# Reordered first loads, a longer last projection chunk and a shorter store wait in a one-core attention kernel

## Chip, cores, metric

One core of a Trainium2 chip. The metric is the device time of one launch in microseconds (us); several runs are timed, and the median is quoted unless something else is said. Each run has a state; every run told here was "fast", and no slow run enters a comparison. A run lists the span of its core and the mean clock granted to TensorE (PE). The time is the span plus 1.8 us. PE is TensorE, ACT ScalarE, DVE VectorE, POOL GpSimd, SP SyncE. K0, V0, K1 and so on are the K and V loads of head 0, 1 and so on; a slice is the part of Wq for one head; to evacuate is to copy a finished matmul result out of PE's accumulation banks (psA, psF, psO).

## The reference

```python
xn = layernorm(A_x)                                   # [2048, 512]
q  = xn @ wq                                          # 32 heads of 128
p  = softmax(q @ k_cache^T * 128**-0.5)               # per head, 2048 keys
s  = (p @ v_cache).concat_heads() @ wo
h  = relu(xn @ w1 + b1)**2 ;  g = silu(h @ w2 + b2)   # 1792 hidden
out = A_x + s * g
```

## The kernel before

Four query blocks of 512 rows; in each, 32 heads; in each head, 8 pairs of key tiles, 1024 pairs in all. One pair is two score matmuls (512 columns), one exponential on ACT (1.02 us) and, two pairs later, eight PV matmuls (probabilities times V, 129 columns). Between them PE gets "fillers": projections of q, the MLP and the output projection, dealt out by a credit that spreads them evenly. Loads are issued in program order by the engine that is named; SP has one queue for nearly all of them. Parts that matter (cuts marked):

```python
CH.append([(0, HC), (HC, 2 * HC), (2 * HC, 2 * HC + 4), (2 * HC + 4, H)])  # head chunks of the last block
...
ln_load(0, 0); ln_load(0, 1, AC); ln_load(0, 2); ln_load(0, 3, AC)  # x tiles, SP and ACT
fill_v(0)                       # SP
fill_wq(0, AC)
fill_k(0)                       # SP, DMA transpose
... fill_wq(1, AC); fill_wq(2, AC)
... # layernorm of 4 tiles, transposes, q of head 0
fill_k(1); fill_v(1)            # SP
for i, (c0, c1) in enumerate([(0, 4), (4, 8), (8, 11), (11, 14)]):
    ... # four pieces of W1, SP
tok_b1 = S.emit_dma(GP, ...)    # biases, issued on POOL
tok_b2 = S.emit_dma(GP, ...)
t_b1 = E(DV, partial(_copy, out=b1f[:], in_=b1b[:]), deps=[tok_b1])   # DVE waits here for b1
...
for pi in range(NPAIR):
    g, k = divmod(pi, NPR)
    gen_scores(pi)
    most = 4 if pi < 2 else 3 if k == 2 else 2      # fillers at most
    ... # fillers
    if pi >= LAG: gen_pv(pi - LAG)
    if k == 0:
        fill_wq(g + 3); fill_k(g + 2)               # at pair 0: the slice of head 3, on SP
    ...
S.emit_wait(GP, fin)            # POOL and SP both wait for the stores
S.emit_wait(SP, fin)
```

The softmax here doesn't subtract the row's maximum and nothing guards it: scores larger than these inputs give would overflow.

## Time and profile before

| | before |
|---|---|
| median (first three runs) | 1256.98 us, 1256.71 to 1257.76 |
| the profiled run | 1259.58 us, span 1257.8, granted clock 0.995 |
| PE busy | 99% of the span |

In the timeline of the kernel before (start, length of the issue, queue, line, operation, count), SP's queue holds behind K0 and K1 (the two transposes) four W1 pieces, and behind these a slice of Wq:

```profile
2.12 9.67 SPq L220 DMA_TRANSPOSE kT<-in_A_k_cache_dram  x2
...
12.46 4.76 SPq L216 DMA_DIRECT2D w_sb<-in_B_w_dram  x4
...
17.26 0.91 SPq L216 DMA_DIRECT2D wq_sb<-in_A_wq_dram  x1
```

The last line is the fourth slice, for head 3. Nobody waited for it, because PE was held up earlier by W1.

### The profile page before, as it was taken

What the parts mean: (1) busy time and instruction counts of PE and PEld (TensorE: products, weight loads), DVE (VectorE), ACT (ScalarE), POOL (GpSimd) and SP (SyncE); (2) the same over time, 40 slices, a digit from 0 to 9 for tenths busy, and PEclk for the clock granted to TensorE, in tenths of its full rate; (3) what the DMA queues carried; (4) which work ended last, traced back from release to release, by engine and by line L of the source; (5) the groups of instructions that cost most, each with busy time, mean ns of one, the idle gap of its engine ahead of it and who ended that gap; (6) DMA issues with size and microseconds to landing.
All of it is one profiled execution on the core that took longest, in us unless ns stands there. A gap on an engine that the chain in (4) does not pass through costs nothing.

```text
span 1257.8 us, 26666 instructions
## 1 busy us (share of the span) xinstructions
PE 1240.5 (99%) x11772; PEld 812.8 (65%) x11755; DVE 471.9 (38%) x946; ACT 1056.8 (84%) x1047; POOL 33.7 (3%) x78
## 2 busy tenths in 40 slices
PE   7999999999999999999999999999999999999996
PEld 3666666666666666666666666666666666666664
DVE  2543332344434333334443433233354333233342
ACT  4888888888888888888888888888888888888893
POOL 2001000000001000000000100000000000000000
PEclk8999999999999999999999999999999999999998
DMA  9999977787788887877878798787777797777760
GB/s 206 207 221 199 175 144 133 131 148 141 128 159 155 156 146 142 144 131 136 141 144 147 158 171 139 133 151 136 134 148 139 144 171 140 129 146 142 133 120 26
DMA packets 686835, 185.39 MB, mean 147 GB/s; under 512 B 675168, under 2 KB 685792, under 8 KB 686720
## 3 DMA queue, kind: packets, MB, share of 16 engines
q1 hardware_dynamic: 683408, 179.23, 78.3%
q0 software_dynamic: 1440, 3.81, 1.2%
q8 instruction: 93, 1.52, 0.5%
q10 hardware_dynamic: 1872, 0.66, 0.2%
q14 instruction: 22, 0.18, 0.1%
HBM read 96.08 MB, written 2.10 MB: 78 GB/s over the span
## 4 chain that ended last, share of the span: by engine, by line
PE 97%; DMA 1%; SPq 1%; DVE 0%; issue 0%
PE psO L157 37%; PE psA L152 35%; PE psF L152 25%; SPq L220 1%; DMA w_sb<-in_B_w_dram 1%; DMA oT<-o_bf 0%; SPq L216 0%; DVE o_un L179 0%; DVE o_bf L165 0%; DVE tmp_t L175 0%; DVE out_t L165 0%; DVE rden L191 0%
## 5 line engine op out<-in xcount | busy, mean ns | idle before, releaser
L161 ACT ACTIVATE pT<-psA 128x1024 bf16<-128x1024 f32 x1024 | 1045.4, 1024 | 177.6 <-PE psA L152 131.4
L157 PEld LDWEIGHTS psO<-v_sb,pT 128*128 128x128 bf16 x8192 | 549.3, 98 | 245.7 <-issue 17.1
L157 PE MATMUL psO<-v_sb,pT 128*128 128x129 bf16 x8192 | 635.5, 220 | 0.0
L152 PE MATMUL psA<-qt_sb,kT 128*128 128x512 bf16 x2048 | 610.0, 379 | 1.0 <-DMA kT<-in_A_k_cache_dram 1.0
L179 DVE COPY o_un<-psO 128x258 f32<-128x258 f32 x256 | 97.2, 421 | 404.9 <-PE psO L157 404.7
L152 PE MATMUL psF<-wo_all,oT 128*128 128x512 bf16 x488 | 167.9, 381 | 4.3 <-DMA oT<-o_bf 4.3
L152 PE MATMUL psF<-xnT,wq_sb 128*128 128x512 bf16 (+1 forms) x524 | 168.6, 374 | 0.2 <-ACT xnT L161 0.2
L152 PEld LDWEIGHTS psA<-qt_sb,kT 128*128 128x128 bf16 x2048 | 158.5, 98 | 1.7 <-DMA kT<-in_A_k_cache_dram 1.2
L179 DVE CAST qt_sb<-psF 128x512 bf16<-128x512 f32 (+1 forms) x129 | 88.2, 684 | 111.4 <-PE psF L152 111.4
L165 DVE TENSOR_TENSOR o_bf<-o_un,rden 128x512 bf16<-128x512 f32 x128 | 88.5, 691 | 4.9 <-DVE rden L191 0.6
L152 PEld LDWEIGHTS psF<-xnT,wq_sb 128*128 128x128 bf16 x524 | 50.7, 98 | 60.7 <-ACT xnT L161 0.3
L152 PEld LDWEIGHTS psF<-wo_all,oT 128*128 128x128 bf16 x488 | 47.7, 98 | 62.4 <-DMA oT<-o_bf 5.3
L171 DVE TENSOR_SCALAR r_t<-psF,b1f 128x512 bf16<-128x512 f32 x56 | 41.9, 748 | 109.3 <-PE psF L152 109.3
L152 PE MATMUL psF<-xnT,w_sb 128*128 128x512 bf16 x224 | 78.5, 385 | 4.4 <-DMA w_sb<-in_B_w_dram 4.4
L152 PE MATMUL psF<-w_sb,h2T 128*128 128x512 bf16 x224 | 74.3, 379 | 0.0
L152 PEld LDWEIGHTS psF<-xnT,w_sb 128*128 128x128 bf16 x224 | 22.0, 99 | 31.6 <-DMA w_sb<-in_B_w_dram 4.9
L152 PEld LDWEIGHTS psF<-w_sb,h2T 128*128 128x128 bf16 x224 | 21.9, 98 | 26.4
L165 DVE TENSOR_TENSOR acc<-psF,acc 128x512 f32<-128x512 f32 x32 | 22.0, 688 | 37.8 <-PE psF L152 37.8
L165 DVE TENSOR_TENSOR z_t<-psF,b2bc 128x512 f32<-128x512 f32 x16 | 11.1, 692 | 60.9 <-PE psF L152 60.9
L216 POOL DMA_DIRECT2D out_dram<-out_t x12 | 6.8, 565 | 889.2 <-DVE out_t L165 889.2
L165 DVE TENSOR_TENSOR h2T<-r_t 128x512 bf16<-128x512 bf16 x56 | 23.8, 425 | 1.9
L191 DVE RECIPROCAL rden<-o_un 128x4 f32<-128x4 f32 x128 | 22.8, 178 | 4.4
(41 smaller groups left out, 147.4 us busy)
## 6 DMA issues: line engine op xcount, KB each, us to landing
v_sb<-in_A_v_cache_dram SPq DMA_DIRECT2D x128, 512.0 KB, 4.8
wq_sb<-in_A_wq_dram SPq DMA_DIRECT2D x125, 128.0 KB, 3.2
wo_all<-in_A_wo_dram SPq DMA_DIRECT2D x4, 1024.0 KB, 6.3
kT<-in_A_k_cache_dram SPq DMA_TRANSPOSE x128, 4.6
oT<-o_bf SPq DMA_TRANSPOSE x128, 3.9
x_t<-in_A_x_dram POOLq DMA_DIRECT2D x16, 128.0 KB, 3.6
x_ln<-in_A_x_dram SPq DMA_DIRECT2D x14, 128.0 KB, 2.8
w_sb<-in_B_w_dram SPq DMA_DIRECT2D x1, 1792.0 KB, 10.3
```

The lines of the kernel that those rows point to most:

```text
L152: return e.matmul(out, lhsT, rhs, start=start, stop=stop)
L157: return e.matmul(out, lhsT, rhs, start=start, stop=stop, skip_group_check=True)
L161: return e.activation(out, in_, func, bias=bias, scale=scale)
L165: return e.tensor_tensor(out, in0, in1, op)
L171: return e.tensor_scalar(out, in0, scalar1=scalar1, scalar2=scalar2, op0=op0, op1=op1)
L179: return e.tensor_copy(out, in_)
L191: return e.reciprocal(out, in_)
L216: return e.dma_start(out, in_)
L220: return e.dma_start(out, in_, transpose=True)
```

## The change

Its intent: K0 is what the first scores need, so it goes first on SP; W1's first piece comes ahead of K1 and V1; the first pairs no longer touch W1. At the end, 16 heads in the last chunk leave 22 matmuls that don't need the last head, to be done while its output is normalized and transposed. Only SP waits for the stores. Cut to its core:

```diff
-    CH.append([(0, HC), (HC, 2 * HC), (2 * HC, 2 * HC + 4), (2 * HC + 4, H)])
+    CH.append([(0, HC), (HC, 2 * HC), (2 * HC, H)])
...
-        t = E(GP, partial(_ts, out=ve_t[:, i:i + 1], ...
+        t = E(DV if j == 0 else GP, partial(_ts, out=ve_t[:, i:i + 1], ...
...
-            jobs.append((k, k - 130, job_h(j, c), None))
+            jobs.append((k, max(k - 130, 4), job_h(j, c), None))
...
+    n_in, n_after = 14, 22
+    n2 = n_in + n_after - 2 * (nt - 1)
+    tail_order = [(i, x) for i in range(2) for x in range(nt - 1)] + [(2, x) for x in range(n2)]
...
-        if tok_oT[(NQB - 1) * H + CH[-1][-1][0] + x] is None:
+        if step < NPAIR and step < NPR * ((NQB - 1) * H + CH[-1][-1][0] + x + 1) + 10:
             return False
...
     ln_load(0, 0)
-    ln_load(0, 1, AC)
-    ln_load(0, 2)
-    ln_load(0, 3, AC)
-    fill_v(0)
+    for i in range(1, TPB):
+        ln_load(0, i, AC)
+    fill_k(0)
     fill_wq(0, AC)
-    fill_k(0)
...
+    fill_v(0)
+    fill_wq(1)
+    fill_wq(2)
+    load_w1(0)
+    fill_k(1)
+    fill_v(1)
+    for i in range(1, 4):
+        load_w1(i)
...
-        most = 4 if pi < 2 else 3 if k == 2 else 2
+        most = 0 if pi == 0 else 4 if pi == 1 else 3 if k == 2 else 2
...
-    S.emit_wait(GP, fin)
     S.emit_wait(SP, fin)
```

Left out: the loads are taken out of their old places further down, the warm-up matmuls load their weights each time, and q of head 0 is evacuated as three tiles and one instead of two and two.

More of the change, by code (lines that the diff above doesn't have):

```diff
@@ L179, in _copy @@
     return e.tensor_copy(out, in_)
-def _mm_keep(e, out, lhsT, rhs, start, stop):
-    return e.add_instruction(mybir.InstMatmult(
-        start_tensor_calc=start, stop_tensor_calc=stop, ldweights=False,
-        name=e.bass.get_next_instruction_name(), engine=e.engine,
-        ins=[e.lower_ap(rhs), e.lower_ap(lhsT)], outs=[e.lower_ap(out)]))
 def _recip(e, out, in_):
@@ L361, in ln_stats @@
         t = E(DV, partial(_bn_aggr, out=mv_t[:, i, :], in_=st_t[:, i, :]), deps=[t])
-        t = E(GP, partial(_ts, out=ve_t[:, i:i + 1], in0=mv_t[:, i, 1:2], scalar1=1.0,
-                          scalar2=LN_EPS, op0=ALU.mult, op1=ALU.add), deps=[t] + prev)
+        t = E(DV if j == 0 else GP,
+              partial(_ts, out=ve_t[:, i:i + 1], in0=mv_t[:, i, 1:2], scalar1=1.0,
+                      scalar2=LN_EPS, op0=ALU.mult, op1=ALU.add), deps=[t] + prev)
         t_xr[jt] = E(GP, partial(_tt, out=rstd[:, i:i + 1], in0=ve_t[:, i:i + 1], in1=mhalf[:],
@@ L410, in first_proj @@
         for c in range(NDC):
-            t = E(PE, partial(_mm, out=bankF(i // 2)[:, i * P:(i + 1) * P], lhsT=wq_sb[:, 0, c, :],
+            t = E(PE, partial(_mm, out=bankF(i // 3)[:, i * P:(i + 1) * P], lhsT=wq_sb[:, 0, c, :],
                               rhs=xnT[:, c, i * P:(i + 1) * P], start=(c == 0),
@@ L417, in first_evac @@
     def first_evac(i, n):
-        t_evac[0] = t_bankF[i // 2] = E(
+        t_evac[0] = t_bankF[i // 3] = E(
             DV, partial(_copy, out=qt_sb[:, 0, i * P:(i + n) * P],
-                        in_=bankF(i // 2)[:, i * P:(i + n) * P]), deps=[t_proj[0]])
+                        in_=bankF(i // 3)[:, i * P:(i + n) * P]), deps=[t_proj[0]])
     def warm_up(n):
-        for i in range(n):
-            E(PE, partial(_mm_keep if i else _mm, out=bankF(1), lhsT=warm[:, 0:P], rhs=warm[:], start=True,
+        for _ in range(n):
+            E(PE, partial(_mm, out=bankF(1), lhsT=warm[:, 0:P], rhs=warm[:], start=True,
                           stop=True), deps=[t_warm], inc=False)
@@ L757, in bass_recurrent_scan__mha_block_cached__dense_activation_squared_relu__prompt_kernel @@
     tail.append(job_wo(NQB - 1, m, TPB - 1, half, D))
-    tail_order = [(0, x) for x in range(nt - 1)] + [(1, x) for x in range(nt - 3)]
-    tail_order += [(0, nt - 1)] + [(1, x) for x in range(nt - 3, nt)]
-    tail_order += [(i, x) for i in range(2, TPB + 1) for x in range(nt)]
+    n_in, n_after = 14, 22
+    n2 = n_in + n_after - 2 * (nt - 1)
+    tail_order = [(i, x) for i in range(2) for x in range(nt - 1)] + [(2, x) for x in range(n2)]
+    tail_order += [(0, nt - 1), (1, nt - 1)] + [(2, x) for x in range(n2, nt)]
+    tail_order += [(i, x) for i in range(3, TPB + 1) for x in range(nt)]
     tail_place = {}
@@ L778, in tail_one, with load_w1 @@
         return True
-    ln_load(0, 0)
-    ln_load(0, 1, AC)
-    ln_load(0, 2)
-    ln_load(0, 3, AC)
-    fill_v(0)
-    fill_wq(0, AC)
-    fill_k(0)
-    E(AC, partial(_act, out=th_t[:, 0, 0:1], in_=warm[:, 0:1], func=ACT.Exp), deps=[t_warm])
-    fill_wq(1, AC)
-    fill_wq(2, AC)
+    w1_view = B_w1.rearrange("(c p) f -> p c f", p=P)
+    tok_w1 = [None] * 4
+    def load_w1(i):
+        c0, c1 = [(0, 4), (4, 8), (8, 11), (11, 14)][i]
+        tok_w1[i] = S.emit_dma(
+            SP, partial(_dma, out=w1_sb[:, :, c0 * P:c1 * P], in_=w1_view[:, :, c0 * P:c1 * P]),
+            sl_w1[i])
+    ln_load(0, 0)
+    for i in range(1, TPB):
+        ln_load(0, i, AC)
+    fill_k(0)
+    fill_wq(0, AC)
+    E(AC, partial(_act, out=th_t[:, 0, 0:1], in_=warm[:, 0:1], func=ACT.Exp), deps=[t_warm])
+    fill_v(0)
+    fill_wq(1)
[5 more added lines that the diff above has]
+        load_w1(i)
     for i in range(TPB):
@@ L807, in bass_recurrent_scan__mha_block_cached__dense_activation_squared_relu__prompt_kernel @@
     first_proj(1)
-    first_evac(0, 2)
     first_transpose(3)
@@ L811, in bass_recurrent_scan__mha_block_cached__dense_activation_squared_relu__prompt_kernel @@
     first_proj(2)
+    first_evac(0, 3)
     first_proj(3)
-    first_evac(2, 2)
-    fill_k(1)
-    fill_v(1)
-    w1_view = B_w1.rearrange("(c p) f -> p c f", p=P)
-    tok_w1 = [None] * 4
-    for i, (c0, c1) in enumerate([(0, 4), (4, 8), (8, 11), (11, 14)]):
-        tok_w1[i] = S.emit_dma(
-            SP, partial(_dma, out=w1_sb[:, :, c0 * P:c1 * P], in_=w1_view[:, :, c0 * P:c1 * P]),
-            sl_w1[i])
+    first_evac(3, 1)
     tok_b1 = S.emit_dma(GP, partial(_dma_gather, nc, out=b1b[:],
@@ L844, in bass_recurrent_scan__mha_block_cached__dense_activation_squared_relu__prompt_kernel @@
         at(j * SPB + SPB // 2, partial(load_xt, j))
-    left = [sum(job[0] for _, _, job, _ in jobs) + 14]
+    left = [sum(job[0] for _, _, job, _ in jobs) + n_in]
     credit = 8.0
```

## The prediction

> **What bounds the kernel now.** I read the page's engine table first, then the waits of TensorE for the whole run, then the two ends in the timeline and the table by stage, because the diff touches only the first 25 us and the last 30 us.
>
> ```profile
> PE 1240.5 (99%) x11772; PEld 812.8 (65%) x11755; DVE 471.9 (38%) x946; ACT 1056.8 (84%) x1047; POOL 33.7 (3%) x78
> PE 97%; DMA 1%; SPq 1%; DVE 0%; issue 0%
> ```
>
> TensorE is busy 99% of the span and makes 97% of the chain of waits; between 40 and 1220 us the view of waits lists no PE wait at all. A 512-column matmul takes one slot of 0.216 us there (two score matmuls are 0.43 us of the chain, eight PV matmuls 0.45). So the middle can only shrink if matmuls go away, and none does: the change has the same columns to multiply. What can be won is PE idle time and half-clock time at the ends. The table by stage shows these (columns: stretch, length, busy time and count of PE, PEld, DVE, ACT, POOL, then granted clock, DMA share, GB/s):
>
> ```profile
> 12.00:15.00 3.00, 2.97 (x14) 1.29 (x14) 0.00 (x0) 2.05 (x2) 0.00 (x0) 1.00 1.21 176
> 15.00:18.80 3.80, 0.23 (x2) 0.00 (x0) 1.36 (x3) 1.02 (x1) 0.00 (x0) 1.00 1.25 252
> 18.80:25.60 6.80, 5.92 (x29) 3.42 (x30) 1.18 (x2) 1.58 (x2) 0.00 (x0) 0.50 1.16 308
> 1233.70:1235.30 1.60, 0.07 (x2) 0.01 (x1) 0.00 (x0) 1.16 (x2) 0.00 (x0) 1.00 0.43 82
> 1240.30:1244.15 3.85, 1.51 (x10) 0.55 (x7) 1.63 (x4) 0.00 (x0) 0.00 (x0) 1.00 0.18 34
> 1244.15:1247.57 3.42, 3.01 (x8) 1.08 (x9) 1.75 (x3) 0.00 (x0) 1.26 (x1) 0.50 0.00 0
> ```
>
> Two holes, each followed by a stretch at half clock. The timeline names what ended each idle spell (start, length, what, idle before it and its releaser):
>
> ```profile
> 12.03 0.60 PE L152 MATMUL psA<-qt_sb,kT 128*128 128x512 bf16 x2 [1.04 <-DMA kT<-in_A_k_cache_dram]
> ...
> 19.68 0.61 PE L152 MATMUL psF<-xnT,w_sb 128*128 128x512 bf16 x1 [4.45 <-DMA w_sb<-in_B_w_dram]
> ...
> 1235.30 0.60 PE L152 MATMUL psF<-wo_all,oT 128*128 128x512 bf16 x2 [1.53 <-DMA oT<-o_bf]
> ...
> 1244.56 1.89 PE L152 MATMUL psF<-wo_all,oT 128*128 128x512 bf16 x4 [2.75 <-DMA oT<-o_bf]
> ```
>
> PE waits for K of head 0, then for W1, then twice for a transposed head output. A third piece is after the last matmul: the program's last result is written at 1253.19 and the span ends at 1257.8. The instructions of line 134 (the end of the block) show why:
>
> ```profile
> L134 POOLq DRAIN  x1: 2519/2519/2519, 1255.0 to 1255.0; - x1
> L134 SPq DRAIN  x1: 7/7/7, 1255.0 to 1255.0; - x1
> L134 POOLq EVENT_SEMAPHORE  x2: 17/17/17, 1257.6 to 1257.7; - x2
> ```
>
> POOL starts a drain of 2.52 us only at 1255.0, because it first waits for the last store (1254.8), and the others wait for POOL at 1257.6.
>
> [...] clock 0.50 from 18.77 to 25.60 us, after the 4.45 us hole, and from 1244.15 to 1247.57 us (3.41 us). [...] The chain here has 0.85 to 0.87 us for two such matmuls at 20 us and 0.43 us at 30 us. [...] K of head 0, queued behind V, took 9.9 us to land against a median of 4.6. [...] No run shows yet that an earlier drain is equally short.
>
> **The change part by part.**
>
> *Prologue, W1 hole.* Before, from the first score (12.03) PE has 14 matmuls of 512 columns to do, 14 x 0.216 = 3.02 us, so it is done at 15.07 and idle until 19.68: 4.6 us. Then it runs at half clock until 25.60, which loses half of 5.92 us, 2.96 us. Loss 7.57 us. After, SP queues K0, V0, two weight slices, the first W1 piece, and only then K1, V1. Bytes up to and including that W1 piece: x 0.52, K0 0.52, V0 0.52, three slices 0.39, W1 0.52, together 2.5 MB. Between 2 and 16 us the stages moved about 200 GB/s on average, which lands W1 near 2 + 12.3 = 14.3 us; at the 285 GB/s of the stage 2 to 4 us, near 11. No H matmul is allowed before pair 4 now. With the first score at 11.0: two score pairs 0.87, three projection matmuls 0.65, a short wait for the first exponential (about 11.6 + 1.02), then pairs 2 and 3, PE-bound, to about 15.5, and the pair-4 scores to 16.0. So W1 is there in time and the hole is gone, with about 0.2 us of idle waiting for the first exponential. Gain 7.57 - 0.2 = 7.4.
>
> *Prologue, first score.* It started at 12.03, when K0 landed; q was ready at 11.03 + 0.42 = 11.45. K0 now goes out right after the first x tile, near 1.15 us. Its own 0.52 MB and the x tiles and slice beside it, 1.2 MB at 200 to 285 GB/s, land between 6.2 and 8 us. So q sets the start. Moving the variance operation from POOL (0.19 us and its gap, 0.27 per tile, in a chain where POOL is the busy one) to DVE brings tile 1 forward by about 0.35 us and tiles 2 and 3 by 0.65 and 0.9 us; later links (ACT copies of 0.6 us, PE transposes) eat part. I follow tile 3: scaled 8.7, transposed 9.65, copied 10.1, projected 10.5, then a last copy of 128 columns in place of 256, perhaps 0.3. q ready near 10.95. Gain about 1.0. Warm-up matmuls now reload their weights; loads overlap PE (cold loads of 0.15 us inside slots of 0.43), and the warm-up ends at 6.5 against 6.7 for the first normalized tile: 0.
>
> *Tail.* The last chunk has 16 heads instead of 4 + 12. The 16 matmuls of the 4-head chunk leave the loop, and 22 matmuls instead of 6 stand between the last PV and the first that needs head 127. Columns are the same. Before, counted as losses against a PE at full clock: 1.53 waiting for head 126 inside the loop; 1244.56 less (1240.36 + 6 x 0.216) = 2.9 waiting for head 127; half of the 3.0 us from 1244.56 to 1247.57, 1.5. Sum 5.9. After: the rule that a head's matmul comes 10 steps after its last pair takes head 126 out of the loop; 22 x 0.216 = 4.75 us cover the 4.2 us (1240.31 to 1244.51) of evacuation, normalization and transposing, so no hole, no half clock. Cross-check by time: loop shorter by 16 x 0.216 + 1.53 = 4.98; from last PV to last matmul 4.75 + 28 x 0.216 = 10.8 against 11.98, 1.2 less; sum 6.2. I take 6.0.
>
> *Stores.* POOL's last addition ends some 1.5 us before the last matmul; its drain then ends about 1.1 us after that matmul, the last store lands 2.5 us after it. SP alone goes 1254.79 -> 1255.03 -> exchange of signals 0.2. End near 1255.28 in old times, gain 2.45.
>
> Sum: 7.4 + 1.0 + 6.0 + 2.45 = 16.85. 1256.98 - 16.85 = 1240.1.
>
> **Rivals.** *K0 slows the x tiles:* three of them now queue on ACT beside K0's small packets. For it: [...] DMA is fully used from 2 us on. Against it: x tile 3 is not needed before 6.6 us, when DVE has done three tiles, and landed at 4.3. If it held, q would come 1 to 3 us late: 1241 to 1243. *V0, a weight slice or W1 still lands late*, as the transpose may hold up what is behind it on SP: K0's issue took 6.79 us before, K1's only 2.83. If the long form returns behind x, V0 goes out at 8 and W1 near 10, landing at 16 to 17: one or two us of hole, perhaps the clock with it: 1242 to 1245. *ACT becomes the bound at the start or near the end:* an exponential takes 1.02 us, a pair without filler 0.88 us of PE. Pair 0 has no filler now, and the gated tail may leave others without. For whole stretches it can't be: 1418 fillers over 1024 pairs give 0.88 + 1.385 x 0.216 = 1.18 us. It would cost 1 us: 1241. *The drain stays:* if POOL's 2.5 us depend on the stores or on the end of the other engines, nothing is won there: 1242.5.
>
> **Range and chances.** The holes are seen in the trace and the fillers are counted, so I give the sum most weight; each rival alone costs 1 to 5 us, and few things can make it better than the sum (q earlier, at most 2 us). Range 1237.5 to 1245. Two per cent is 25 us, more than all idle and half-clock time found (about 20 with the drain), so faster by over 2% gets 0.01; a new stall of over 40 us would be needed for slower, 0.01; within 2%, 0.98.
>
> **What would show it.** First score near 11.0 with q, not K, as releaser; no PE wait for W1 and clock 1.00 from 5 us to the end of the matmuls; no PE wait for the transposed output, 22 output matmuls between the last PV and the one that needs head 127; POOL's drain begun before the last store lands, span end about 0.5 us after it. I am wrong if a K, V or weight wait of over 1 us appears between 10 and 25 us, if the clock drops anywhere, or if POOL's drain still ends last.

That POOL's drain moves forward when it starts earlier, on which the 2.45 us rest, was at that time the author's assumption.

## The result

1246.34 us (1245.36 to 1247.62, 4 runs) against 1257.36 (1256.71 to 1257.76, 4 runs): ratio 0.9913, 95% interval 0.9896 to 0.9931. A ratio is the mean time of one kernel's fast runs over that of the other's of the same rounds, so it is not quite the ratio of the medians. The kernel is 11.0 us faster; I had said 16.85 (from 1256.98) and a range of 1237.5 to 1245.0. The class (within 2%) was right, the size was not.

The page of the changed kernel, same lines as before:

```profile
span 1245.2 us, 26489 instructions
...
PE 1226.2 (98%) x11568; PEld 814.4 (65%) x11776; DVE 471.0 (38%) x946; ACT 1057.1 (85%) x1047; POOL 32.9 (3%) x74
...
PE 97%; SPq 1%; issue 1%; DMA 1%; ACT 0%; DVE 0%
```

PE is the bound as before. Its matmul count is not to be read: some records are missing from this trace, while the weight loads (PEld) are all there.

The table by stage of the changed kernel, with the columns of the prediction's table:

```profile
15.00:22.20 7.20, 6.64 (x60) 3.96 (x58) 3.28 (x6) 5.12 (x5) 0.00 (x0) 1.00 1.17 262
22.20:24.50 2.30, 0.11 (x2) 0.01 (x1) 0.44 (x2) 1.02 (x1) 0.00 (x0) 1.00 1.30 138
24.50:25.62 1.12, 1.12 (x12) 0.76 (x13) 0.00 (x0) 0.00 (x0) 0.00 (x0) 1.00 1.22 274
25.62:29.04 3.42, 3.42 (x19) 2.04 (x18) 1.85 (x5) 1.66 (x2) 0.00 (x0) 0.50 1.07 214
...
1231.40:1236.20 4.80, 4.76 (x23) 2.17 (x23) 1.43 (x4) 0.00 (x0) 0.00 (x0) 1.00 0.14 27
1236.20:1242.30 6.10, 6.02 (x44) 4.10 (x42) 4.54 (x7) 0.00 (x0) 2.53 (x2) 1.00 0.12 43
```

The tail is full and at full clock, as predicted. The prologue still has a hole, later and shorter (22.2 to 24.5), and a half-clock stretch after it; the prediction had named both as signs that it is wrong. The timeline of the changed kernel names what ended the hole, and shows that the tail's matmuls follow each other without a wait:

```profile
24.50 0.39 PE L152 MATMUL psF<-xnT,wq_sb 128*128 128x512 bf16 x1 [2.19 <-DMA wq_sb<-in_A_wq_dram]
...
1231.44 3.40 PE L152 MATMUL psF<-wo_all,oT 128*128 128x512 bf16 x15
1234.67 1.46 PE L152 MATMUL psA<-wo_all,oT 128*128 128x512 bf16 x6
1235.97 0.59 PE L152 MATMUL psF<-wo_all,oT 128*128 128x512 bf16 x2
```

(The weight loads in the tail are x16, x6 and x2: the predicted 22 stand before the first that needs the last head, and one record of the 16 matmuls is missing.) So PE now waits for the fourth slice of Wq. In the view of that tile, one issue of the slice (issue length, start) and its time to landing, in the changed kernel:

```profile
L208 SPq DMA_DIRECT2D wq_sb<-in_A_wq_dram x1: 543/543/543, 17.3 to 17.3; - x1
DMA to landing us min/median/max: 7.1/7.1/7.1
```

It is issued at 17.3 and lands 7.1 us later, at 24.45. In the kernel before it landed at 24.16. What SP's and ACT's queues together have to move up to that slice is the same in both kernels; only the order ahead of it changed.

The instructions at the block's end in the changed kernel:

```profile
L134 POOLq DRAIN  x1: 3837/3837/3837, 1240.3 to 1240.3; - x1
...
L134 SPq DRAIN  x1: 7/7/7, 1245.0 to 1245.0; - x1
```

POOL's drain runs from 1240.3 to 1244.1, before SP has seen the last store. It is recorded as 3.84 us; a POOL addition of 1.27 us (1240.33 to 1241.60) runs in the same time.

Following the start of the exponential of each pair through both traces tells when the gain came and went. The changed kernel is ahead by 0.8 us at pair 0, by 8.6 us at pair 4 (so what I had added up was there), by 7.7 at pair 8, by 5.5 at pair 9, and by 3.6 to 3.9 from pair 10 to pair 100 (later the lead grows, as 16 matmuls have left the loop). The drop to pair 9 is the wait for the slice, that to pair 10 the half clock.

### The profile page after: what moved, and what is told of

It is laid out like the page before. It is cut to its first block, busy times and chain, and to the rows that moved or that the text cites. A ratio compares the mean times of both kernels' runs of the same rounds, so it can differ in the third digit from the quotient of the medians.

```text
span 1245.2 us, 26489 instructions
## 1 busy us (share of the span) xinstructions
PE 1226.2 (98%) x11568; PEld 814.4 (65%) x11776; DVE 471.0 (38%) x946; ACT 1057.1 (85%) x1047; POOL 32.9 (3%) x74
## 4 chain that ended last, share of the span: by engine, by line
PE 97%; SPq 1%; issue 1%; DMA 1%; ACT 0%; DVE 0%
PE psO L157 37%; PE psA L152 35%; PE psF L152 24%; SPq L208 1%; DMA wq_sb<-in_A_wq_dram 1%; SPq L212 1%; ACT pT L161 0%; DVE tmp_t L175 0%; DVE out_t L165 0%
## 5 line engine op out<-in xcount | busy, mean ns | idle before, releaser
L152 PE MATMUL psA<-qt_sb,kT 128*128 128x512 bf16 x1853 | 567.3, 379 | 10.9 <-DVE qt_sb L179 0.7
L152 PE MATMUL psF<-wo_all,oT 128*128 128x512 bf16 x479 | 164.1, 379 | 0.1
L165 DVE TENSOR_TENSOR acc<-psF,acc 128x512 f32<-128x512 f32 x28 | 19.3, 689 | 35.9 <-PE psF L152 35.9
```

The costliest lines, as they stand in the source:

```text
L152: return e.matmul(out, lhsT, rhs, start=start, stop=stop)
L165: return e.tensor_tensor(out, in0, in1, op)
```

## The experiments

Twelve runs were made, in three groups of four (ten new kernels, one of them twice, and the changed kernel again); each group shares the runs of the kernel before on its chip. All were correct.

**wq3_early.** Theory A: the gain is given back because a small slice stands last in SP's queue. Theory B: there are too many bytes, whatever their order.

```diff
     load_w1(0)
+    fill_wq(3)
     fill_k(1)
...
-            fill_wq(g + 3)
+            if g > 0:
+                fill_wq(g + 3)
```

> The changed kernel with one load moved: the fourth slice of Wq (for head 3), which is issued on SP behind all of W1, K1 and V1 and lands at 24.45 us, is issued right after the first W1 piece. Theory A (the gain in the prologue is given back because this small slice stands last in SP's queue): it lands before 15 us, the PE wait for wq_sb of 2.2 us at 24.5 us is gone, the clock stays 1.00, and the time falls from about 1246.3 us by 2.2 to 3.9 us, to 1242.4 to 1244.1, with less spread between runs. Theory B (the loads of the first 25 us are simply too many bytes, whatever their order): a wait of about the same length appears on another load (a later W1 piece, K or V of head 1 or 2), and the time stays within 1 us of 1246.3.

The profiled run bears out A: the slice lands at 14.4, no PE wait for it between 11 and 40 us, clock 1.00, and no W1, K or V wait in its place; it took 1244.46 us. But the four other runs took 1247.39 to 1251.35, median of all five 1248.61, ratio 0.993 [0.9917, 0.9944]: not faster than the changed kernel, and with a spread of 7 us. The expected time was missed, and A alone does not explain that.

**pool_waits.** The one line back.

```diff
+    S.emit_wait(GP, fin)
     S.emit_wait(SP, fin)
```

> The changed kernel with one part undone: POOL too waits for the stores at the end. Theory: POOL's drain is 2.5 us of its own work, so it starts again after the last store and the time rises by 2.4 us, to about 1248.8; the drain is the last thing that ends. Rival: the drain's end depends on the other engines or on the stores, so that waiting costs nothing, and the time stays within 0.5 us of 1246.3.

At the block's end of this kernel:

```profile
L134 POOLq DRAIN  x1: 2519/2519/2519, 1245.0 to 1245.0; - x1
...
L134 SPq EVENT_SEMAPHORE  x1: 17/17/17, 1247.7 to 1247.7; - x1
```

SP is through with the stores at 1244.8, as in the changed kernel, but the end comes at 1247.7 instead of 1245.1: 2.5 us in the trace. The times, 1248.17 (1247.57 to 1249.5), are only 1.3 to 1.8 us above the two medians of the changed kernel (1246.34 and 1246.87); runs of either kernel vary by 2 us, so the times confirm the direction and the trace gives the size.

**old_tail.** The chunks, the order and the rule of the kernel before, in the changed kernel.

```diff
-    CH.append([(0, HC), (HC, 2 * HC), (2 * HC, H)])
+    CH.append([(0, HC), (HC, 2 * HC), (2 * HC, 2 * HC + 4), (2 * HC + 4, H)])
... # tail_order, the rule in tail_one and the count of held matmuls as before
```

> The changed kernel with the tail of the kernel before (chunks of 4 and 12 heads, 6 matmuls held back). Theory: the two PE waits for the transposed head output (1.5 and 2.8 us) and the half-clock stretch come back, so it takes 5.5 to 6.2 us longer, about 1252.3. Rival: the tail's waits were mostly covered by something else and the trace only counts them twice; then it takes less than 4 us longer, under 1250.3.

The waits of this kernel after 1215 us (who, for what, total, times, longest) have the tail's waits again; the changed kernel has none:

```profile
PE psF L152 <- DMA oT<-o_bf: 4.3, 2, 2.8
```

1252.63 us (1251.63 to 1253.74): 5.8 to 6.3 us above the two medians of the changed kernel, as expected. By the profiled spans (1250.3 against 1245.2) and by the ratios it is 5.1 us, a little under. Both are well over the rival.

**old_prologue.** The kernel before with the new tail and the shorter store wait (its prologue is the one shown above, unedited).

> The kernel before with the new tail and with SP alone waiting for the stores, its prologue untouched. Theory A: the prologue part of the change is worth only what the two traces differ by at pair 20, 3.8 us, or less (some runs of either kernel have a half-clock window more or less), so this kernel takes 1248.5 to 1250.2 us. If the prologue were worth the 8.4 us that I predicted, this kernel would take about 1254.7.

1250.10 us (1248.86 to 1250.74), as theory A says: the change's prologue is worth 3.2 to 3.8 us by the medians, 2.6 us by the ratios (0.9935 against 0.9914, the mean of the two ratios of the changed kernel), not 8.4. PE's waits between 11 and 40 us in this kernel are the old ones:

```profile
PE psF L152 <- DMA w_sb<-in_B_w_dram: 4.5, 1, 4.5
PE psA L152 <- DMA kT<-in_A_k_cache_dram: 1.1, 1, 1.1
```

**after_again.** The control for the spread.

> The changed kernel itself once more, beside the three below on the same chip. It is the control for the spread: 1245.3 to 1247.7 us as in its first four runs, in two groups about 1.7 us apart (with and without one half-clock window after the wait for the fourth Wq slice).

1246.87 us (1246.67 to 1247.72, 4 runs), ratio 0.9916. Not two groups this time: three runs lie within 0.3 us, and one, at clock 0.999, 0.8 us above them. Its profile has the same 2.2 us wait for the slice, but no half-clock stretch. So the drop of the clock after this hole is there in some runs and not in others. What decides is not shown. What the traces give is this. In the trace before, half clock runs from 18.77 to 25.60 and from 1244.15 to 1247.57 us, in that of the changed kernel from 25.62 to 29.04 (up to the last matmul); within each trace these changes lie whole multiples of 3.413 us apart, by its own record of the clock. In the 3.41 us just ahead of the three drops PE was idle for 3.4, 2.3 and 2.2 us. Laid out in such stretches, the changed kernel's wait falls into one (first line, PE busy for 1.22 of 3.41 us), the control's into two, with PE idle for 0.7 and 1.4 us and the clock at 1.00:

```profile
22.21:25.62 3.41, 1.22 (x13) 0.77 (x13) 0.43 (x2) 1.02 (x1) 0.00 (x0) 1.00 1.28 182
...
21.08:24.49 3.41, 2.67 (x25) 1.49 (x22) 1.58 (x3) 2.75 (x3) 0.00 (x0) 1.00 1.57 304
24.49:27.90 3.41, 1.97 (x21) 1.38 (x22) 0.00 (x0) 0.98 (x2) 0.00 (x0) 1.00 0.73 166
```

**wq3_early_again.**

> The same kernel as wq3_early, whose profiled run took 1244.46 us while its timed runs took 1247.4 to 1251.4. Theory A (it was disturbed by chance): 1243.5 to 1245.5 us now, with a spread as small as the control's. Theory C (this order of loads has a wait that is there in some runs and not in others): the spread of several us is there again, and a profile of a slow run shows which wait it is.

1246.27 to 1250.70, median 1247.91: theory C. This time the profile fell on a slower run (1249.52). The wait for the slice is down to nothing, but PE has another, of 3.7 us, for the evacuation of q by DVE, and the clock is 0.50 from 19.3 to 26.1 us. The next kernel gave the same picture.

**wq3_before_w1rest.** The slice one place further back than in wq3_early, so that K1 and V1 keep theirs.

```diff
     fill_v(1)
+    fill_wq(3)
     for i in range(1, 4):
         load_w1(i)
```

> The changed kernel with the fourth Wq slice issued after V1 and before the last three W1 pieces (so K1 and V1 keep their places). Theory A: the slice lands near 19 to 20 us, before it is needed at 22, the hole of 2.2 us and the half-clock window go, and the time is 2.2 to 3.9 us under the control's slower group, 1242.5 to 1244.5. Theory B (too many bytes): a wait for a W1 piece comes instead and the time stays within 1 us of the control.

Two groups: 1242.93, 1243.15, 1243.99, 1244.40 (clock 1.00), as A says, and 1248.55, 1250.30 (clock 0.997). The profiled run is of the slower group. DVE's timeline in it:

```profile
18.89 0.17 DVE L179 CAST b1f<-b1b 128x14 f32<-128x14 bf16 x1 [7.90 <-DMA b1b<-in_B_b_dram]
18.97 1.28 DVE L179 CAST qt_sb<-psF 128x512 bf16<-128x512 f32 x2
```

DVE stood 7.9 us before the conversion of the bias b1, with two evacuations of q behind it; PE needed a bank that these free, as its timeline in the same run says:

```profile
19.80 1.01 PE L152 MATMUL psF<-xnT,w_sb 128*128 128x512 bf16 x2 [3.50 <-DVE qt_sb L179]
```

What the DMA engines did while b1 was awaited is in the table by stage of this run (last two columns: DMA share and GB/s):

```profile
14.00:16.00 2.00, 2.00 (x23) 1.32 (x21) 0.00 (x0) 1.60 (x2) 0.00 (x0) 1.00 1.19 81
16.00:18.00 2.00, 0.29 (x2) 0.00 (x0) 0.00 (x0) 1.06 (x2) 0.00 (x0) 1.00 1.13 93
18.00:20.00 2.00, 0.20 (x1) 0.13 (x2) 1.11 (x3) 0.00 (x0) 0.00 (x0) 0.60 1.36 227
```

From 14 to 18 us the DMA engines have a mean busy share of 1.19 and 1.13 (1.30 in the two microseconds before) and move 81 and 93 GB/s (188 before). In this stretch the load of the bias b1, issued by POOL at 8.5 us, and K1's transpose, issued by SP at 9.2, are both under way: b1 lands 10.4 us after its issue, K1 10.6. In the profile of the changed kernel K1 was issued at 8.66 and b1 at 8.87; they landed after 8.2 and 7.1 us, and the DMA engines moved 123 GB/s from 14 to 16 us and 214 from 16 to 18. That the two loads hold each other up was the author's guess.

**wq3_late.** The suspected wait made longer.

```diff
             fill_k(g + 2)
+            if g == 0:
+                fill_wq(3)
```

> The suspected wait made longer: the fourth Wq slice issued behind K2 as well. It should land 2 to 3 us later, near 27 us; theory A: the PE wait at pair 9 grows by as much, and the time rises by 2 to 4.5 us over the control, to 1248 to 1251. If this wait were not on the path, the time would not change.

The slice lands at 28.0, and the wait grows to match. PE's timeline:

```profile
28.08 0.39 PE L152 MATMUL psF<-xnT,wq_sb 128*128 128x512 bf16 x1 [4.24 <-DMA wq_sb<-in_A_wq_dram]
```

1249.90 us (1248.96 to 1253.47), 3.0 above the control, for 2.0 us more of wait and half-clock time in every run. The wait for the slice is on the path.

**b_on_sp.** Theory D: the slow group comes from the bias loads and K1 being under way together (the collision). On wq3_before_w1rest, both bias loads go to SP's queue ahead of K1.

```diff
     load_w1(0)
+    tok_b1 = S.emit_dma(SP, partial(_dma_gather, nc, out=b1b[:], ...
+    tok_b2 = S.emit_dma(SP, partial(_dma, out=b2bc[:], ...
     fill_k(1)
... # the two on POOL removed
```

> wq3_before_w1rest with the two bias loads taken off POOL and issued on SP just ahead of K1. The slow profile of wq3_before_w1rest shows K1 and the bias loads from POOL's queue in flight together from 13 to 19 us, both slowly (b1 lands at 18.9 instead of 15.9 to 17.4, and DVE stands before the conversion of b1 with the evacuation of q behind it, so PE waits 3.5 us and the clock drops for 6.8 us). Theory D (this collision is the cause of the slow group): [...] the slow group is gone, and all runs lie between 1241.5 and 1244.5 us. Rival E (the slow group comes from something else, for instance the first tiles [...]): runs of 1247 to 1250 us appear among the five again.

1243.84 us (1243.22 to 1247.20). Three runs are where D puts all five, one is at 1245.27, and one at 1247.20 with clock 0.997. So D's "all" fell. The profile is of a faster run (b1 at 15.4, K1 at 17.6, no PE wait of over 0.8 us up to 60 us); what held up the slow one is not known.

**b_first.** The same two loads on POOL, ahead of everything, so that they meet K0 instead of K1.

```diff
+    tok_b1 = S.emit_dma(GP, ...
+    tok_b2 = S.emit_dma(GP, ...
     ln_load(0, 0)
... # the two further down removed
```

> wq3_before_w1rest with the two bias loads issued on POOL at the very start, so that they fall beside K0 and the x tiles rather than K1. Theory D: K1 is undisturbed and no run shows the wait before the b1 conversion, but the collision may now slow K0 and the x tiles, so the first score comes at 11.2 to 14 us: 1242 to 1246 us, no run at 1248 or more from a wait for b1. Rival E: slow runs as before.

1243.38 us (1242.78 to 1243.86, 4 runs, all at clock 1.00), ratio 0.9886 [0.9869, 0.9904]: the best kernel and the steadiest. The price is there too: K0 lands at 10.0 instead of 8.05, and the first exponential starts at 12.7 instead of 11.8. But K1 lands 6.0 us after its issue (10.6 in wq3_before_w1rest), b1 had landed at 9.3, before that issue, and the stages in which wq3_before_w1rest moved 81, 93 and 227 GB/s have 261, 225 and 247:

```profile
14.00:16.00 2.00, 2.00 (x17) 1.15 (x16) 0.69 (x1) 1.60 (x3) 0.00 (x0) 1.00 1.23 261
16.00:18.00 2.00, 2.00 (x23) 1.41 (x22) 0.69 (x1) 1.71 (x2) 0.00 (x0) 1.00 0.99 225
18.00:20.00 2.00, 1.95 (x18) 1.17 (x17) 0.93 (x2) 1.41 (x3) 0.00 (x0) 1.00 1.09 247
```

**b_on_sp_x_first.** On b_on_sp, the x tiles and the first slice ahead of K0.

```diff
     ln_load(0, 0)
-    for i in range(1, TPB):
-        ln_load(0, i, AC)
+    ln_load(0, 1, AC)
+    ln_load(0, 2)
+    ln_load(0, 3, AC)
+    fill_wq(0)
     fill_k(0)
-    fill_wq(0, AC)
```

> b_on_sp, and the four x tiles and the first Wq slice ahead of K0 (x0, x2 and the slice on SP, x1 and x3 on ACT), so that ACT's queue holds nothing beside K0's transpose. In the changed kernel the fourth x tile lands at 6.7 to 8.7 us against 4.3 before. Theory F [...]: tile 3 lands before 5 us, K0 not later than 9.6, the first exponential starts at 11.5 to 11.9 us in the profile and the time is 0 to 1.5 us under b_on_sp, 1241 to 1242.5. Rival: K0, now issued 0.9 us later, lands later by more than that and is waited for; then it is as slow as b_on_sp or slower.

Everything that was expected of the trace came: tile 3 at 4.24, K0 at 8.03, first exponential at 11.63. The time did not: 1243.90 us (1243.00 to 1245.64), no better than b_on_sp. The profiled spans differ by 0.4 us (1241.5 and 1241.9), less than the runs of either kernel do: the start gained 0.2 us against b_on_sp's profile (11.81), and a wait of 0.8 us for a Wq slice stands against one of 0.3 (PE's waits up to 60 us).

**cast_late.** On wq3_early, DVE's conversion of b1 moved to just before its first use; no load is moved.

```diff
         def evac(bank, step):
+            nonlocal t_b1
+            if t_b1 is None:
+                t_b1 = E(DV, partial(_copy, out=b1f[:], in_=b1b[:]), deps=[tok_b1])
             s = c % 2
```

> wq3_early (10 runs of it: 1244.5 to 1251.4 us, median 1248.3) with the DVE conversion of b1 moved to just before its first use, behind the evacuations of q; the loads are untouched. It keeps the collision and takes away what DVE's order makes of it. If the PE hole comes from DVE standing before b1, it shrinks from 3.5 us to under 1.5 and the clock stays at 1.00: 1243 to 1246.5 us. If the late K1 and V1 themselves are what PE waits for, the times stay spread from 1244 to 1251.

1245.89 us (1243.84 to 1247.09), against 1244.5 to 1251.4 in ten runs of wq3_early. In its profile both loads land late (b1 at 19.8, K1 at 20.5), and still PE has no wait of over 0.7 us for q up to 40 us and the clock stays at 1.00. So the long hole comes from the order on DVE. Two waits of 1.3 us for later slices remain (at 34 and 63 us); that the late K1 causes them was not shown.

## Why the prediction was wrong

*Tail, 6.0 us predicted.* Right in mechanism, size nearly: no wait for the transposed output, clock 1.00, 10.85 us from the last PV to the last matmul (predicted 10.8). Undoing it costs 5.1 us in span, 5.8 to 6.3 by the medians.

*Stores, 2.45.* Right: 2.5 us in the traces with and without POOL's wait. Started early, the drain is recorded as 3.84 us; less the 1.27 us of the addition in the same time that is 2.57 (an estimate), against 2.52 for the late one, which the prediction had left open. (POOL's last addition ends 0.6 us before the last matmul in the trace before, not 1.5; this changed nothing.)

*First score, 1.0.* Right in the profile of the changed kernel: 0.84 us, with q as the releaser. But the control, the same kernel, starts its first exponential at 13.33, later than the kernel before (12.68). In the ten profiles with these first loads (all but the kernel before, old_prologue, b_first and b_on_sp_x_first) it starts between 11.76 and 13.47, on average at 12.4: a gain of 0.3 us, not 1.0. In the five that start after 12.4, DVE waited 1.1 to 2.1 us for x tile 3; in the other five at most 0.4. The control's DVE:

```profile
8.58 0.69 DVE L200 BATCH_NORM_STATS2 st_t<-x_ln 128x6 f32<-128x512 bf16 x1 [1.94 <-DMA x_ln<-in_A_x_dram]
```

So what the rival "K0 slows the x tiles" feared did come, and in half of the profiles it was not small: tile 3 landed between 5.50 and 8.70 in these ten, at 4.3 in the kernel before, and at 4.24 where it went ahead of K0 (b_on_sp_x_first, one profile). This is the second term that was mis-sized.

*W1 hole, 7.4. This is the step that failed.* Its own terms held: W1's first piece landed at 12.84, well before it was needed, and at pair 4 the kernel was 8.6 us ahead. What failed is the sentence "the hole is gone". I summed the bytes up to the W1 piece and stopped there. Behind it in the same queue stood the fourth Wq slice, whose place and landing (24.16 us) could be read in the trace before. With PE some 8 us earlier, that landing became the next wait. The loss in the changed kernel is 2.2 us of hole, and half of 3.41 us, 1.7, when the clock drops. Two of the first four runs lie 1.4 to 2.3 us above the other two; the two slower ones have a granted clock of 0.999, the two faster ones 1.000, as one stretch of 3.41 us at clock 0.50 in 1245 us would give (0.9986). Of these runs only one, a slower one, was profiled. On average, then, about 3.0 us. That the wait is on the path is shown by wq3_late (+2.0 us of wait, +3.0 us of time) and by the faster runs of wq3_before_w1rest.

*The base of the sums.* 16.85 us were read off a run of 1259.58 us and taken from 1256.98. Runs of the kernel before lie between 1254.20 (clock 0.999) and 1260.75 (0.995), so half-clock stretches come and go; one of 3.41 us at clock 0.50 costs up to half of it, 1.7 us (an estimate). The profiled run was one with more of them than the median run (the same W1 wait of 4.5 us was followed by 6.8 us of half clock in it and by 3.4 us in old_prologue's profile). That is worth 1259.58 - 1257.36 = 2.2 us, which the change could not win from the median.

Together: 3.0 + 2.2 = 5.2 of the 5.8 us by which the gain was overstated. The first score, 0.7 us short of its term on average, would cover the other 0.6; that the runs that were not profiled spread alike is not shown. A wait of 0.5 us for DVE's evacuation of q (at 16.9 us) was not tested in the changed kernel either.

*Readings that were off, without effect on the outcome.* The 0.87 us that the prediction gives for two 512-column matmuls at 20 us is that of eight PV matmuls; two took 0.85. Its own figures for the stores give 2.5 us (1257.8 less 1255.28).

*The rival that I named* ("V0, a weight slice or W1 still lands late") had the right kind of wait, but its reason was wrong: K0's issue did not last 6.8 us this time but 2.65, and all three that I meant came early.

A check from the other side: with both waits out of the way, b_first stands 0.49% below old_prologue by the ratios (0.9886 against 0.9935), which is 6.2 us. That is what the prologue was worth: 8.4 less one half-clock stretch of 3.41 us that the median run may not have had (1.7) is 6.7.

*Left open:* whether K1's transpose and the bias loads of POOL's queue slow each other, and why they took 10.6 and 10.4 us to land in one profile and 8.2 and 7.1 in another; what decides whether the clock drops after the 2.2 us wait; why x tile 3 lands late in some runs; and the slow run of b_on_sp. The advantage of b_first over b_on_sp rests on four and five runs and isn't settled.

## What to carry to other kernels

When a load is moved forward, list everything that shares its queue, with landing times and the time at which each will be needed after the gain; the next wait is often a load that nobody waited for, because something else was late first. A small load that is needed soon should not stand behind large ones that are needed later (here the slice, 2.2 us of wait), and a conversion of a late operand should not stand ahead of evacuations on the same engine (here b1, 3.5 us of wait for PE). Compare the profiled run's own time with the median before subtracting what its trace shows.
